# The guard of a chunk selection as a step of its own, and a new order for all steps

## The chip, the cores and the metric

The kernel runs on one core of a Trainium2 chip. The metric is the device time of one execution in microseconds; a profile of one execution shows what each engine did. The engines are TensorE (PE, with its weight loads as PEld), VectorE (DVE), ScalarE (ACT), GpSimd (POOL) and SyncE (SP, which here only issues transfers). Each works through its own queue of instructions in order and waits where an instruction needs something that another engine has not finished.

## The reference

Attention in which each query looks only at the six best chunks of 32 keys, followed by a normalised gated feed-forward layer. Batch 4, 8 heads, 768 positions, head dimension 64; model dimension 512, hidden dimension 1536:

```python
k_chunks = k.reshape(B, H, nc, chunk, D)          # 24 chunks of 32
k_min, k_max = np.min(k_chunks, axis=3), np.max(k_chunks, axis=3)
ub = np.sum(np.maximum(q[:, :, :, None, :] * k_min[:, :, None, :, :],
                       q[:, :, :, None, :] * k_max[:, :, None, :, :]), axis=-1)
ub = np.where(causal, ub, -1e9)
top_chunks = np.argsort(ub, axis=-1)[..., -6:]
scores = np.where(sel & causal_positions, scale * q @ k.T, -1e9)
x = softmax(scores) @ v                            # heads side by side: 3072 x 512
xn = x / rms(x) * rms_g
g, val = xn @ w_gate, xn @ w_val
out = (g * sigmoid(g) * val) @ w_out
```

## The kernel before, in words

**Tiling.** The 32 heads are taken as 16 pairs (two heads fill the 128 partitions). A pair goes through `prep`: q and k are loaded (qload, kload; `qnat`, `knat`), turned by TensorE (qT, kT, line 517) and copied out of PSUM (qE, kE, by ACT or DVE). DVE takes each chunk's maximum and minimum of k (kmx, kmn, lines 546 and 548), their difference is taken (dif, 599), the positive part of q is taken (relu, 633 on ACT or 635 on DVE), and TensorE forms the bounds (ub, 723 or, for two pairs at once, 781), which are copied out (ubE), turned back (up) and masked (ubm).

**Selection.** Function `choose`: twelve MAX8 instructions (max, line 650) give the eight largest bounds of each query; the sixth is the threshold. `pick` (step sel) writes, into 25 columns, whether each of 24 chunks beats the threshold (lines 665, 674), and in the 25th the guard: the largest bound minus 480, not under zero (lines 668, 679). Both instructions are one step on DVE. For the first three pairs (a0, a1, a2) the 25 columns stand in a tile `selq` and are turned by TensorE (selT, 694) and copied into the tile `qs` (selC); for later pairs they stand in `qn` beside a bf16 copy of q (qN, on GpSimd) and both are turned by a transposing transfer (qX, line 557). The columns of k that face them are constants, so that one matmul gives the score plus the mask.

**Attention and the feed-forward part.** Scores (sc, 868) go through the exponential on ACT (exp, 885), for batches 1 to 3 through a causal mask on GpSimd (mask, 891), then to the product with v (av, 904), which DVE normalises (xb, 924 and 925). Every half batch of 384 rows is normalised (`norm`: sq, eps, root, xs, then tp and tpE, or transfers xT) and multiplied by the gate weights (gate, line 1037), the value weights (val, 1058) and the output weights (po, 1078), with tanh on ACT (1044) and two DVE instructions for each of the twelve hidden slices (tg 1050, hh 1066). poE copies the output out and out stores it.

**What sets the order.** Nothing is scheduled when the kernel is built. `PROGRAM` is a string written out ahead: each word names the engine (P, A, D, G, S), the number of the step, and the buffer slots it opens. `Order.run` gives each step that engine and slot, and the steps are emitted in that sequence, so each engine's queue is the words with its letter. The durations given to `add` only served the search that wrote the string. Steps named busy (line 338) are optional: matmuls on a tile of zeros, of which the string holds 34, the first 12 in front of TensorE's first transpose. GpSimd's queue also issues the loads of v and of the weights (wg, wv, wo, lines 437 and 442).

In PROGRAM the first pairs' steps are known by number only; here they are named by the kind of step and the pair, as relu of a4. Each pair has a set (tiles `ke` and `qs`), of which there are three; a pair's copies of k into `ke` (kC) wait until the scores of the set's earlier pair are done.

Of the kernel before, what the change touches and what calls it, by code (L numbers as in the profile page):

```python
# [21 lines left out]
GUARD = 480.0  # L22
# [176 lines left out]
def kernel(  # L199
# [83 lines left out]
    def pe(n):  # L283
        return 0.003 + n / 2400.0
# [56 lines left out]
    for i in range(BUSY):  # L341
        bank = Buf("ps")
        add("busy", "PE", pe(4 * P), 1000.0 + i, busy(bank, 4 * P), [c_zero], opens=[bank])
# [135 lines left out]
    def prep(c, i0, nb, at, lr):  # L479
# [162 lines left out]
        def choose(last, ubm, m8):  # L642
# [43 lines left out]
            if side_q:  # L686
                c.sel = turned(QN, qn, QS, "qX", [pk, qs_n])
                return c.sel
# [461 lines left out]
```

## Time and profile before

| | |
|---|---|
| median of 3 runs | 315.69 us (314.5 to 319.53) |
| the profiled execution | 314.75 us, span 313.0 us |
| PE busy | 303.2 us (97%) |
| DVE busy | 231.5 us (74%) |
| ACT busy | 185.5 us (59%) |
| GpSimd busy | 103.9 us (33%) |
| mean granted TensorE clock | 0.997 |

The span runs from the first to the last instruction; the time of the execution has a little around it. In the timeline rows the first number is the start in us, the second the length of the run of instructions, and what stands in brackets is the idle time of the engine before it and who ended it. In the rows of groups the number behind x is the count; behind the bar stand the busy time in us, the mean of one in ns, and the idle time in front of the group. Busy time of matmuls is partly modelled: one matmul's end overlaps the next one's start, so spacing is the better price.

### The profile page before, as it was taken

The page shows a single profiled execution, that of the slowest core. Times are in us where ns is not written, and L with a number is a line of the kernel's source. Part 1 is how long each engine was busy: PE and PEld are TensorE (multiplying, and loading weights), DVE is VectorE, ACT ScalarE, POOL GpSimd, SP SyncE. Part 2 cuts the span into 40 slices and gives each one's busy share as a digit, 9 for nine tenths or more (in the row PEclk, how much of TensorE's full clock was granted, in tenths as well). Part 3 has the DMA queues.
Part 4 walks back from the last instruction along what each step waited for, and adds up shares of the span by engine and source line. Part 5 has one row for each costly group of instructions (what it writes and reads, how often), then busy time and mean ns, then how long its engine had stood idle before and what let it go on. Part 6 is the DMA issues. An engine that isn't in the chain of part 4 may idle for free.

```text
span 313.0 us, 7431 instructions
## 1 busy us (share of the span) xinstructions
PE 303.2 (97%) x2772; PEld 191.7 (61%) x2790; DVE 231.5 (74%) x654; ACT 185.5 (59%) x415; POOL 103.9 (33%) x162
## 2 busy tenths in 40 slices
PE   7998999999999999999999999999999999999994
PEld 3676776576576855667687546656666545555541
DVE  4998989969985789856978879989544564577551
ACT  1688998783298773697794643366697403442001
POOL 8686453371354843252377100033233110000000
PEclk9999999999999999999999999999999999999998
DMA  9999999999699996797684060361240034100014
GB/s 173 220 190 126 96 191 206 201 165 168 129 185 198 220 114 146 175 191 138 138 68 28 17 140 13 52 77 36 58 79 36 2 78 155 69 3 0 2 67 169
DMA packets 113301, 35.35 MB, mean 113 GB/s; under 512 B 106225, under 2 KB 110065, under 8 KB 113265
## 3 DMA queue, kind: packets, MB, share of 16 engines
q1 hardware_dynamic: 83152, 26.62, 41.1%
q0 software_dynamic: 28512, 7.87, 24.9%
q10 hardware_dynamic: 1600, 0.39, 0.6%
q8 instruction: 22, 0.36, 0.5%
q14 instruction: 15, 0.11, 0.1%
HBM read 28.57 MB, written 6.29 MB: 111 GB/s over the span
## 4 chain that ended last, share of the span: by engine, by line
PE 87%; DMA 5%; DVE 4%; POOL 1%; issue 1%; SPq 1%; ACT 1%; POOLq 0%
PE po L1078 20%; PE vp L1058 19%; PE gp L1037 19%; PE sc L868 9%; PE av L904 5%; DMA wv<-in_moe_w_val_dram 4%; PE pk L517 3%; PE busy L338 3%; PE pq L517 3%; PE ub L781 2%; PE ub L723 2%; PE up L803 1%; DMA qs<-qn 1%; DVE m L650 1%; DVE qs L293 1%
## 5 line engine op out<-in xcount | busy, mean ns | idle before, releaser
L885 ACT ACTIVATE pt<-sc 128x512 bf16<-128x512 f32 (+2 forms) x192 | 92.9, 561 | 17.5 <-PE sc L868 15.4
L1044 ACT ACTIVATE sg<-gp 128x384 bf16<-128x384 f32 x96 | 45.5, 496 | 55.1 <-PE gp L1037 42.2
L1050 DVE SCALAR_TENSOR_TENSOR tg<-sg,gp 128x384 bf16<-128x384 bf16 x96 | 51.8, 550 | 32.0 <-ACT sg L1044 30.6
L1058 PE MATMUL vp<-xT,wv 128*128 128x384 bf16 x384 | 74.0, 326 | 0.3 <-DMA wv<-in_moe_w_val_dram 0.2
L1037 PE MATMUL gp<-xT,wg 128*128 128x384 bf16 x384 | 73.2, 326 | 0.7 <-ACT xT L289 0.4
L1078 PE MATMUL po<-wo,hh 128*128 128x512 bf16 x272 | 66.9, 379 | 0.9 <-issue 0.2
L1066 DVE TENSOR_TENSOR hh<-vp,tg 128x384 bf16<-128x384 f32 x96 | 51.6, 552 | 12.6 <-PE vp L1058 11.7
L868 PE MATMUL sc<-qs,ke 128*128 128x128 bf16 (+5 forms) x420 | 57.1, 251 | 0.3 <-DMA qs<-qn 0.2
L1058 PEld LDWEIGHTS <-wv 128*128 128x128 bf16 x384 | 35.9, 98 | 25.0 <-issue 1.2
L1037 PEld LDWEIGHTS <-wg 128*128 128x128 bf16 x384 | 36.2, 98 | 23.9 <-issue 1.5
L1078 PEld LDWEIGHTS <-hh 128*128 128x128 bf16 x288 | 27.3, 98 | 29.1 <-issue 1.5
L904 PEld LDWEIGHTS <-pt 128*128 128x128 bf16 x672 | 35.1, 98 | 10.5 <-ACT pt L885 0.6
L904 PE MATMUL av<-vx,pt 128*128 128x65 bf16 x672 | 41.4, 193 | 0.1
L891 POOL TENSOR_SCALAR_AFFINE_SELECT pt<-pt 128x512 bf16<-128x512 bf16 (+1 forms) x48 | 24.4, 521 | 47.4 <-ACT pt L885 43.6
L868 PEld LDWEIGHTS <-ke 128*128 128x128 bf16 (+1 forms) x420 | 30.6, 97 | 9.6 <-issue 1.6
L293 POOL CAST ke<-kt 64x768 bf16<-64x768 f32 x32 | 26.6, 835 | 16.6 <-ACT kt L289 6.0
L293 POOL CAST qn<-qnat 128x768 bf16<-128x768 f32 x13 | 10.7, 822 | 40.5 <-DMA qs<-qn 40.5
L291 ACT ACTIVATE osb<-po 128x512 f32<-128x512 f32 x12 | 7.1, 599 | 24.7 <-PE po L1078 24.7
L981 DVE SCALAR_TENSOR_TENSOR xs<-xb,ri,gains 128x512 bf16<-128x512 bf16 x24 | 17.5, 751 | 2.1 <-POOL ri L973 1.7
L925 DVE TENSOR_TENSOR xb<-av,rden 128x384 bf16<-128x384 f32 (+1 forms) x34 | 18.2, 534 | 1.2
L473 POOL DMA_DIRECT2D vx<-in_v_dram x16 | 16.9, 1055 | 0.1
L650 DVE MAX8 m<-ubm 128x8 f32<-128x8 f32 (+4 forms) x192 | 16.7, 160 | 0.2
(83 smaller groups left out, 297.7 us busy)
## 6 DMA issues: line engine op xcount, KB each, us to landing
out_dram<-osb SPq DMA_DIRECT2D x24, 256.0 KB, 2.3
knat<-in_k_dram SPq DMA_DIRECT2D x30, 192.0 KB, 4.3
qnat<-in_q_dram SPq DMA_DIRECT2D x30, 192.0 KB, 4.6
vx<-in_v_dram POOLq DMA_DIRECT2D x16, 192.0 KB, 5.5
wg<-in_moe_w_gate_dram POOLq DMA_DIRECT2D x2, 768.0 KB, 11.6
wv<-in_moe_w_val_dram POOLq DMA_DIRECT2D x2, 768.0 KB, 10.0
wo<-in_moe_w_out_dram POOLq DMA_DIRECT2D x2, 768.0 KB, 10.1
qs<-qn SPq DMA_TRANSPOSE x26, 2.8
```

What stands on the lines that cost most here:

```text
L293: engine[e].tensor_copy(out_, in_)
L650: nc.vector.max(out=m8.tile[:, y[0], y[1], :], in_=ubm.tile[:, y[0], y[1], 0:max(8, 4 * (i0 + x) + 4)])
L868: nc.tensor.matmul(t[:, x:x + m, :].rearrange("p a b -> p (a b)"), ke[kk, kb * P:(kb + 1) * P], qs[kk, q0 * P:(q0 + m) * P], start=not tri ...
L885: nc.scalar.activation(out=t[:, 0:nn, :], in_=sc.tile[:, 0:nn, :], func=ACT.Exp, scale=SCALE)
L891: nc.gpsimd.affine_select(out=pt.tile[:, 0:nd, :], in_=pt.tile[:, 0:nd, :], compare_op=ALU.is_ge, fill=0.0, base=0, pattern=[[0, nd], [1, ...
L904: nc.tensor.matmul(av.tile[:, qi - i0, :], pt.tile[:, x, :], VX[c.v.slot][:, hl * NT + kb, :], start=(begin and m == 0), stop=(left[0] == ...
L1037: nc.tensor.matmul(t[:], wg[:, g, hs], XT[b].tile[:, g, cols], start=(g == 0), stop=(g == NP - 1))
L1044: nc.scalar.activation(out=t[:], in_=gp.tile[:], func=ACT.Tanh, scale=0.5)
L1050: nc.vector.scalar_tensor_tensor(out=t[:], in0=sg.tile[:], scalar=1.0, in1=gp.tile[:], op0=ALU.add, op1=ALU.mult)
L1058: nc.tensor.matmul(t[:], wv[:, g, hs], XT[b].tile[:, g, cols], start=(g == 0), stop=(g == NP - 1))
L1066: nc.vector.tensor_tensor(out=t[:], in0=vp.tile[:], in1=tg.tile[:], op=ALU.mult)
L1078: nc.tensor.matmul(po.tile[:], hhs[ht].tile[:, th * P:(th + 1) * P], wo[:, ht, :], start=(ht == 0), stop=(ht == NHT - 1))
```

## The change

The guard becomes a step (grd) of its own. `pick` keeps the comparison; `guard` writes the 25th column, on ScalarE (relu with a bias tile `cap` holding -480), on GpSimd or on DVE. What turns the selection waits for both steps. The relu of q may also go to GpSimd. PROGRAM is written anew for all steps:

```diff
+    cap = const.tile([P, 1], FP32, name="cap")
+    c_cap = add("cap", "DVE", 0.07, -98, lambda e: nc.vector.memset(cap[:], -GUARD))
...
-                nc.vector.tensor_scalar(out=t[:, 0:n], in0=big["q"].tile[:, 0:n], scalar1=0.0,
+                engine[e].tensor_scalar(out=t[:, 0:n], in0=big["q"].tile[:, 0:n], scalar1=0.0,
                                         scalar2=None, op0=ALU.max)
...
-        rl = add("relu", "", {"DVE": 0.07 + n * 0.00056, "ACT": act(n)}, ...
+        rl = add("relu", "", {"DVE": 0.07 + n * 0.00056, "ACT": act(n), "POOL": pool(n)}, ...
...
-                    nc.vector.tensor_scalar(
-                        out=s12[:, :, NCH:NCH + 1], in0=m12[:, :, 0:1], scalar1=-GUARD,
-                        scalar2=0.0, op0=ALU.add, op1=ALU.max)
...
+            def guard(e):
+                if side_q:
+                    s12 = QN[qn.slot][:, D:D + 2 * NT * P].rearrange("p (t d) -> p t d", d=P)
+                    m12 = m8.tile[:].rearrange("p h i e -> p (h i) e")
+                else:
+                    s12 = SELQ[sq.slot][:, 0:nb].rearrange("p i h e -> p (i h) e")
+                    m12 = m8.tile[:, 0:nb].rearrange("p i h e -> p (i h) e")
+                o, m = s12[:, :, NCH:NCH + 1], m12[:, :, 0:1]
+                if e == "ACT":
+                    nc.scalar.activation(out=o, in_=m, func=ACT.Relu, bias=cap[:, 0:1])
+                else:
+                    engine[e].tensor_scalar(out=o, in0=m, scalar1=-GUARD, scalar2=0.0,
+                                            op0=ALU.add, op1=ALU.max)
+
+            gd = add("grd", "", {"ACT": 0.22, "POOL": 0.25, "DVE": 0.12}, rank(at, b, "sel"), guard,
+                     last + (c_qn if side_q else c_sel) + [c_cap], opens=[qn if side_q else sq], uses=[m8],
+                     port=True)
-            pk = add("sel", "DVE", 0.18 + nb * 48 * 0.00104, ...
+            pk = add("sel", "DVE", 0.09 + nb * 48 * 0.00104, ...
...
-                c.sel = turned(QN, qn, QS, "qX", [pk, qs_n])
+                c.sel = turned(QN, qn, QS, "qX", [pk, gd, qs_n])
...
-            sT = add("selT", "PE", nb * 0.057, rank(at, b, "selT"), sel_turn, [pk, c_idb], ...
+            sT = add("selT", "PE", nb * 0.057, rank(at, b, "selT"), sel_turn, [pk, gd, c_idb], ...
```

Where the two strings give steps to engines differently:

| step | before | after |
|---|---|---|
| guard (16) | with sel on DVE | ACT 3, GpSimd 9, DVE 4 |
| relu (16 pairs) | ACT 12, DVE 4 | ACT 6, DVE 4, GpSimd 6 |
| kE and qE (64) | ACT 46, DVE 18 | ACT 39, DVE 25 |
| ubE (22) | ACT 17, DVE 5 | ACT 12, DVE 10 |
| kC (32) | GpSimd 32 | GpSimd 30, ACT 2 |
| dif (16) | GpSimd 11, DVE 5 | GpSimd 12, DVE 4 |
| selC (3) | DVE 3 | DVE 2, ACT 1 |
| ke0, the constants of the first set | DVE | ACT |
| tpE (6) | ACT 4, DVE 2 | ACT 3, DVE 3 |
| busy on PE | 34, twelve ahead of the first transpose | 26, six ahead of it |

In the early part the new string loads the first half of a0's k ahead of its q; takes the third and the fourth pair's k in the other order; and on GpSimd's queue has, between the load of the fourth pair's v and the first weight load, the guard of a2, qN and two kC of a6, two kC of a3, the relu of a4 and one kC of a4, while the other kC and the qN of a4 stand behind the first three weight loads. Before, that place held qN of a6, kC of a2, both kC of a4 and qN of a4.

More of the change, by code (lines that the diff above doesn't have):

```diff
@@ L634, in relu @@
             else:
-                nc.vector.tensor_scalar(out=t[:, 0:n], in0=big["q"].tile[:, 0:n], scalar1=0.0,
+                engine[e].tensor_scalar(out=t[:, 0:n], in0=big["q"].tile[:, 0:n], scalar1=0.0,
                                         scalar2=None, op0=ALU.max)
-        rl = add("relu", "", {"DVE": 0.07 + n * 0.00056, "ACT": act(n)}, rank(at, b, "relu"), relu, done["q"], opens=[rel],
+        rl = add("relu", "", {"DVE": 0.07 + n * 0.00056, "ACT": act(n), "POOL": pool(n)}, rank(at, b, "relu"), relu, done["q"], opens=[rel],
                  uses=[big["q"]], port=True)
@@ L678, in pick @@
                     op0=ALU.max, op1=ALU.is_gt)
-                nc.vector.tensor_scalar(
-                    out=s12[:, :, NCH:NCH + 1], in0=m12[:, :, 0:1], scalar1=-GUARD,
-                    scalar2=0.0, op0=ALU.add, op1=ALU.max)
-            pk = add("sel", "DVE", 0.18 + nb * 48 * 0.00104, rank(at, b, "sel"), pick,
+            def guard(e):
[14 more added lines that the diff above has]
+                     port=True)
+            pk = add("sel", "DVE", 0.09 + nb * 48 * 0.00104, rank(at, b, "sel"), pick,
                      last + (c_qn if side_q else c_sel), opens=[qn if side_q else sq], uses=[m8, ubm],
@@ L696, in sel_turn @@
                         ident_b[:])
-            sT = add("selT", "PE", nb * 0.057, rank(at, b, "selT"), sel_turn, [pk, c_idb], opens=[st], uses=[sq])
+            sT = add("selT", "PE", nb * 0.057, rank(at, b, "selT"), sel_turn, [pk, gd, c_idb], opens=[st], uses=[sq])
             def sel_out(e):
```

247 rows, old and new, of the table PROGRAM are left out of this document.

## The prediction

> **What bounds the kernel now.** I read the share of busy time first, then the busy time of four stretches cut at the first real matmul, the first gate matmul and the last matmul.
>
> ```profile
> PE 303.2 (97%) x2772; PEld 191.7 (61%) x2790; DVE 231.5 (74%) x654; ACT 185.5 (59%) x415; POOL 103.9 (33%) x162
> ```
>
> ```profile
> 0.00:7.27 7.27, 5.07 (x13) 1.87 (x13) 3.26 (x10) 1.49 (x2) 6.15 (x17) 1.00 0.92 170
> 7.27:51.19 43.92, 42.13 (x568) 31.10 (x569) 39.67 (x121) 37.05 (x83) 25.47 (x39) 1.00 1.16 169
> 51.19:308.94 257.75, 255.96 (x2194) 158.69 (x2209) 188.52 (x525) 146.32 (x329) 72.24 (x107) 1.00 0.59 101
> 308.94:313.00 4.06, 0.05 (x1) 0.00 (x0) 0.00 (x0) 0.60 (x1) 0.00 (x0) 0.76 0.51 190
> ```
>
> After the stretch and its length stand PE, PEld, DVE, ACT and POOL busy. From 51.19 us to the last matmul PE idles 1.79 us of 257.75: there the work of TensorE itself is the limit, and a new order can only tie or lose. The last 4.06 us are the last eviction and its transfer. What an order can win lies before 51.19 us, where PE is kept full partly by fillers, matmuls on zeros (line 338):
>
> ```profile
> 2.20 5.24 PE L338 MATMUL busy<-zeros 128*128 128x512 bf16 x12 [2.20 <-DVE zeros L333]
> 7.27 0.49 PE L517 MATMUL pk<-ident_f,knat 128*128 128x128 f32 x3
> ...
> 8.58 1.46 PE L338 MATMUL busy<-zeros 128*128 128x512 bf16 x6
> ...
> 38.47 0.66 PE L868 MATMUL sc<-qs,ke 128*128 128x128 bf16 x7
> ...
> 40.10 0.40 PE L868 MATMUL sc<-qs,ke 89*128 89x128 bf16 x4 [0.18 <-DMA qs<-qn]
> ...
> 51.19 2.76 PE L1037 MATMUL gp<-xT,wg 128*128 128x384 bf16 x16
> ```
>
> The first twelve fillers take 5.07 us, some 0.42 us each; a later one takes 0.216 us (six in 1.46, the last counted with its modelled end of 0.38). The program has 34, so 22 later ones stand for 4.8 us that PE had nothing to do. Without any filler PE's work is 303.2 - 5.07 - 4.8 = 293.3 us. Put behind a start at 4.8 us (below) and ahead of the tail of 4.06, that is a span of 302.2: no order gets under that, so 10.8 us is all there is to win.
>
> What holds PE back before the gates is the chain of waits:
>
> ```profile
> 34.02 0.52 PE st L694 x6
> 34.55 0.07 issue
> 34.62 0.83 POOL ke L293
> 35.45 1.75 SPq L557
> 37.20 0.05 issue
> 37.25 2.80 DMA qs<-qn
> ...
> 40.25 0.85 POOL qn L293
> ...
> 41.87 0.70 POOL wg L437
> 42.57 11.57 DMA wv<-in_moe_w_val_dram
> ```
>
> Two things hang on the selection here. The transposes of the fourth pair's q with its selection (line 557) leave when DVE has written the selection, and the last scores of the first batch start at 40.10, when they have landed. And GpSimd's cast into the same buffer (qn, 40.25) waits for those transposes and stands in front of the weight loads, so wg leaves at 41.87 and wv, 11.57 us later, is the last thing the first products need. DVE's rows around it:
>
> ```profile
> 31.14 1.00 DVE L650 MAX8 m<-ubm 128x8 f32<-128x8 f32 x12
> ...
> 33.16 0.81 DVE L679 TENSOR_SCALAR selq<-m 128x12 bf16<-128x12 f32 x1
> ...
> 34.23 0.19 DVE L668 TENSOR_SCALAR qn<-m 128x12 bf16<-128x12 f32 x1
> ...
> 44.54 0.36 DVE L925 TENSOR_TENSOR xb<-av,rden 128x192 bf16<-128x192 f32 x1
> ```
>
> DVE is busy 39.67 of 43.92 us there and ACT 37.05: the early stage is bound by these two, in turns, and its length is what I try to size.
>
> **The change part by part.** Only the early stage is summed; steps are named by pair (a0 the first). Prices:
>
> ```profile
> L679 DVE TENSOR_SCALAR selq<-m 128x12 bf16<-128x12 f32 x3 | 2.4, 812 | 0.0
> L668 DVE TENSOR_SCALAR qn<-m 128x12 bf16<-128x12 f32 x13 | 2.9, 225 | 0.0
> L346 DVE MEMSET selq<- 128x384 uint32 x2 | 0.8, 378 | 0.1
> L293 DVE COPY qs<-st 64x768 bf16<-64x768 bf16 x6 | 3.3, 555 | 0.6 <-PE st L694 0.5
> L293 DVE COPY qt<-pq 128x384 f32<-128x384 f32 x9 | 4.9, 551 | 1.8 <-PE pq L517 1.8
> L635 DVE TENSOR_SCALAR rt<-qt 128x768 f32<-128x768 f32 x4 | 2.2, 552 | 0.1
> L599 DVE TENSOR_TENSOR ku<-kmx,ku 128x24 f32<-128x24 f32 x5 | 1.0, 192 | 0.0
> L289 ACT ACTIVATE qt<-pq 128x384 f32<-128x384 f32 x23 | 10.8, 495 | 1.0 <-PE pq L517 0.6
> L633 ACT ACTIVATE rt<-qt 128x768 f32<-128x768 f32 x12 | 10.3, 860 | 2.0 <-PE ub L781 1.7
> L330 ACT ACTIVATE first<-ident_f 128x1 f32<-128x1 f32 x1 | 0.2, 204 | 0.0
> L293 POOL CAST qn<-qnat 128x768 bf16<-128x768 f32 x13 | 10.7, 822 | 40.5 <-DMA qs<-qn 40.5
> L891 POOL TENSOR_SCALAR_AFFINE_SELECT pt<-pt 128x512 bf16<-128x512 bf16 x24 | 15.2, 637 | 21.5 <-ACT pt L885 17.9 <-PE av L904 3.5
> ```
>
> *The guard.* The same small instruction costs 0.812 us in the first pairs and 0.225 later. The three dear ones run while GpSimd does its casts of 0.82 us, so I read the difference of 0.59 as DVE held by GpSimd. The Trainium skill (GPSIMD Engine Reference, Key points) has a rule for it: GpSimd shares its SBUF interfaces with VectorE and contends with DVE instructions that use both ports or have two SBUF inputs. The trace agrees by 0.812 against 0.225, and the rule speaks against giving GpSimd more work; what it would cost is the third rival.
>
> *The start.* In the new order the first k is loaded ahead of q, and 6 fillers instead of 12 stand before its transpose.
>
> ```profile
> 0.81 0.99 SPq L497 DMA_DIRECT2D qnat<-in_q_dram  x2
> 1.84 2.66 SPq L497 DMA_DIRECT2D knat<-in_k_dram  x4
> ```
>
> ```profile
> DMA to landing us min/median/max: 3.5/4.3/5.5
> ```
>
> The landing row is that of knat. The first half of k would be issued at 0.81 instead of 1.84 and land at 4.3 to 6.3; the fillers would end at 2.20 + 6 x 0.42 = 4.7, so its transposes move from 7.27 to between 4.8 and 6.3. The second half is still the fourth load and gains only the fillers ahead. I take 1.4 us for the whole start, between 0 (if the second pair's k, still the fifth load, decides) and 2.4.
>
> *DVE up to the fourth pair's selection* (34.42, the end of the row at 34.23). Gone from this stretch: one memset 0.38, two copies of the first pair's selection that ACT takes 1.11, three dear guards 2.44 (a1 to ACT, a2 to GpSimd, a0 stands apart again and is added below), one cheap guard 0.23 (a3, to ACT): 4.16. Added: the first pair's relu 0.55 and difference 0.19, a small memset 0.11, two evictions of q 1.10, the guard of a0, between 0.225 and 0.812: I take 0.81, the row of the same place. Sum 2.76, net 1.4 earlier (2.0 with the cheap guard). With the start, 2.8 us: selection at 31.6, fourth pair's scores at 37.3 instead of 40.10.
>
> *ACT between its first exponential and the last one that the first norm needs*: 40 exponentials in both orders; one relu (0.86), two evictions of q (0.99) and one of k (about the same 0.5) go, a guard of 0.2 (the row of the smallest activation) comes: 2.15 less. The first pair's selection copies, now ACT's, stand ahead of it and are dearer there than DVE's 1.11; they eat part of the start's 1.4, about 0.5. So ACT is 3.0 earlier, near DVE's 2.8. The guards of a1 and a3 stand among the exponentials and wait for DVE's maxima; the a1 guard stands directly in front of the first exponential, where a late maximum would hold the whole row of them.
>
> *GpSimd up to the weights.* The second cast of q that waited until 40.25 is now behind the weight loads. In front of them stand instead: the guard of a2, one qn cast, four ke casts, the relu of a4 and a ke cast that waits for the third pair's scores. A relu of 128x768 on GpSimd is in no row: the cast of as many elements is 0.82, the masks' 0.637 for 512 gives 0.96 for 768, and twice the cast, 1.64, is the far end I take; under 0.637, the shorter mask, nothing speaks. I take 0.85, beside the cast. A guard is between 0.2 and 0.82. The a2 guard waits for the maxima that ended at 32.14 in the old order, 29.3 by my sum; 0.25 + 0.82 x 6 + 0.85 on top is 35.4. The scores it needs are PE's 24.2 us of work in, reached around 39 us in the old order (the row at 38.47), 36.2 now, and a cast of 0.83 later the weights leave: 37 instead of 41.87. wv lands at about 49.4 instead of 54.14.
>
> *First gate.* The last needed attention output ends at 44.90 (row 44.54) and the gates follow 6.3 us later by an unchanged sequence of squares, root, scaling, four transposes and evictions. 2.8 earlier gives 48.4, and the weights are then there (wg before 47, wv when the third group asks for it at 49.7, which also saves the 0.24 of wait at 54.19). PE has exactly the same 140 real steps before it in both orders, so it can follow.
>
> *The rest.* PE's work is the same. DVE gets seven evictions and five smaller copies more but twelve guards fewer, about nothing in sum; ACT loses six relus and twelve evictions, about 6 us of 146, under PE's cover; GpSimd gains six relus, nine guards and loses two casts, 5.9 us on 103.9, also covered unless DVE is held. On SP's queue the transposes keep their sequence but for pairs that change places, and loads of later pairs shift by a place or two. I allow 0.6 us for new waits beside the 1.79.
>
> Sum: -2.8 - 0.24 + 0.6 = -2.4. The profiled execution took 314.75 us, its span 313.0 and 1.75 around it: 310.6 + 1.75 = **312.3 us**. The median of the runs shown, 315.69, lies 0.94 above the profiled one, and they spread from 314.5 to 319.53, so about 2% is what tells a change from none.
>
> **The rivals.** *The early gain does not arrive.* The loads, not the engines, set the pace: DMA's busy share is 1.16 in the early stretch by the row above, the loads after the fourth come in nearly the old sequence, and a front that is only 1 us earlier then meets the same landings. Or the maxima for the guards come late and hold ACT and GpSimd. For it: the dense DMA row. Against: DVE idles only 4.25 us in that stretch, so it, not the loads, was mostly late. It gives 313.0 + 0.6 + 1.75 = 315.3, between 314 and 317.
>
> *Nearly all fillers close.* The start gains its 2.4 and DVE its 2.0, the 0.24 goes, and the 1.79 of later idle time closes too: 314.75 - 6.4 = 308.3; the floor of 302.2 above is a time of 304.0. For it: a front that long is idle only through fillers. Against: start, DVE, ACT and every later wait must come right at once.
>
> *DVE becomes the bound: slower.* By the shared port each DVE instruction that meets a GpSimd one may take 0.59 more. The place is where DVE is fullest while GpSimd now has relus and guards:
>
> ```profile
> 150.00:200.00 50.00, 49.79 (x438) 31.96 (x439) 43.72 (x109) 30.28 (x68) 16.30 (x24) 1.00 0.42 62
> ```
>
> DVE has 6.28 us to spare there; eleven holdings use it up, and each further one is 0.59 on PE. To be slower than before by 2% (322), the 2.4 gained and 7.25 more must be lost: 16 holdings beyond the spare. Few holdings past it give 316 to 319. For it: the three guards. Against: the 24 scalings with two SBUF inputs lie mostly beside little GpSimd work, and GpSimd is busy a third of the time.
>
> **How the numbers follow.** Forecast 312.3 (310 to 314): 0.47. No gain, 315.3: 0.25. DVE held, 316 and up: 0.18, two thirds of it over 322 or so. Fillers closed, 308.3 (304 to 309): 0.10. The 8-in-10 range is 308.5 to 319.5: about 0.06 is left out below and 0.13 above. Faster by over 2% (under 309.4): 0.10; slower by over 2% (over 322): 0.12; between: 0.78.
>
> **What would show it.** In the new profile: first real matmul near 5 us; the fourth pair's transposes issued near 32; wg issued near 37; first gate at 48 to 49; from there PE idle 2 to 3 us. Wrong if the first gate is still near 51 (the loads decide), if GpSimd's relu is far over 0.85, if scalings or squares on DVE have grown by 0.5, or if PE waits on DVE in the middle stretch.

## The result, and the profile after

The new kernel takes 312.65 us (median; 311.42 to 314.49) against 315.69 for the kernel before in the same series: a ratio of 0.9925, with a 95% interval of 0.9898 to 0.9951. Each ratio here is taken over the runs within 1.5% of their kernel's fastest, so where the runs of a kernel scatter it lies below the ratio of the medians. That is a gain of three quarters of a per cent, within the 2% that is called no change, and beside the forecast of 312.3. The profiled execution took 312.63 us, its span 310.9 against 313.0.

Share of busy time of the new kernel, then four stretches cut as before at the first real matmul, the first gate matmul and the last matmul (after the stretch and its length stand PE, PEld, DVE, ACT and POOL busy):

```profile
PE 300.8 (97%) x2764; PEld 190.4 (61%) x2782; DVE 232.2 (75%) x651; ACT 182.2 (59%) x405; POOL 119.5 (38%) x176
```

```profile
0.00:3.79 3.79, 2.55 (x7) 0.77 (x7) 2.56 (x8) 0.82 (x1) 2.98 (x10) 1.00 0.54 119
3.79:48.99 45.20, 42.61 (x567) 31.14 (x567) 37.88 (x122) 39.88 (x89) 32.56 (x47) 1.00 1.28 184
48.99:307.07 258.08, 255.66 (x2194) 158.46 (x2209) 191.75 (x522) 140.94 (x316) 83.97 (x121) 1.00 0.60 100
307.07:310.90 3.83, 0.02 (x1) 0.00 (x0) 0.00 (x0) 0.60 (x1) 0.00 (x0) 0.95 0.55 203
```

Against the four lengths of before (7.27, 43.92, 257.75, 4.06) the span's 2.1 us come apart as follows: the first real matmul is 3.48 earlier, the way from it to the first gate is 1.28 longer, the rest up to the last matmul 0.33 longer, the tail 0.23 shorter. So by this cut the gain is made at the very start, and a third of it is given back before the gates; what the start carries by itself, an experiment shows below. The timeline of PE in the new kernel shows where:

```profile
1.24 2.74 PE L339 MATMUL busy<-zeros 128*128 128x512 bf16 x6 [1.24 <-DVE zeros L334]
3.79 0.87 PE L520 MATMUL pk<-ident_f,knat 128*128 128x128 f32 x3
...
6.03 0.86 PE L520 MATMUL pq<-ident_f,qnat 128*128 128x128 f32 x3 [0.51 <-DMA qnat<-in_q_dram]
...
20.75 0.52 PE L520 MATMUL pk<-ident_f,knat 128*128 128x128 f32 x3 [1.28 <-DMA knat<-in_k_dram]
...
42.09 0.52 PE L520 MATMUL pk<-ident_f,knat 128*128 128x128 f32 x3 [0.42 <-DMA knat<-in_k_dram]
...
48.99 1.46 PE L1051 MATMUL gp<-xT,wg 128*128 128x384 bf16 x8
51.90 0.82 PE L1072 MATMUL vp<-xT,wv 128*128 128x384 bf16 x4 [1.45 <-DMA wv<-in_moe_w_val_dram]
```

Behind the fillers every wait in these rows is for a load: q of a0, k of a6, k of a5, and 1.45 us for the value weights, where the kernel before waited 0.24. DVE, GpSimd and the transfer queue of SP in the same kernel, around the selection and the weights:

```profile
31.70 0.61 DVE L668 SCALAR_TENSOR_TENSOR qn<-m,ubm 128x288 bf16<-128x288 f32 x1
...
41.75 0.36 DVE L939 TENSOR_TENSOR xb<-av,rden 128x192 bf16<-128x192 f32 x1
```

```profile
31.17 0.82 POOL L294 CAST qn<-qnat 128x768 bf16<-128x768 f32 x1
33.05 3.35 POOL L294 CAST ke<-kt 64x768 bf16<-64x768 f32 x4 [1.06 <-PE sc L888]
36.49 2.14 POOL L638 TENSOR_SCALAR rt<-qt 128x768 f32<-128x768 f32 x1
38.57 0.82 POOL L294 CAST ke<-kt 64x768 bf16<-64x768 f32 x1
39.34 0.82 POOL L440 DMA_DIRECT2D wg<-in_moe_w_gate_dram  x1
```

```profile
32.47 3.31 SPq L560 DMA_TRANSPOSE qs<-qn  x2
35.82 1.17 SPq L500 DMA_DIRECT2D qnat<-in_q_dram  x2
37.04 1.27 SPq L500 DMA_DIRECT2D knat<-in_k_dram  x2
```

The selection of a3 is written at 32.31 (34.42 before), its transposes leave at 32.47, and the last attention output that the first norm needs ends at 42.11 (44.90 before). The relu of a4 on GpSimd takes 2.14 us, not 0.85, and stands in front of the first weight load, which leaves at 39.34. SP issues a5's k by 38.31, one microsecond ahead of the weights. That microsecond turned out to matter. The groups (mean ns of one behind the bar and the busy time):

```profile
L638 POOL TENSOR_SCALAR rt<-qt 128x768 f32<-128x768 f32 x6 | 12.8, 2134 | 10.6 <-ACT qt L290 6.1 <-DVE qt L294 4.3
L638 DVE TENSOR_SCALAR rt<-qt 128x768 f32<-128x768 f32 x4 | 2.7, 674 | 0.0
L691 POOL TENSOR_SCALAR qn<-m 128x12 bf16<-128x12 f32 x8 | 3.5, 434 | 28.5 <-DVE m L653 26.8 <-ACT kt L290 1.7
L689 ACT ACTIVATE qn<-m,cap 128x12 bf16<-128x12 f32 x2 | 0.7, 355 | 0.0
L691 DVE TENSOR_SCALAR qn<-m 128x12 bf16<-128x12 f32 x3 | 0.6, 184 | 0.0
L995 DVE SCALAR_TENSOR_TENSOR xs<-xb,ri,gains 128x512 bf16<-128x512 bf16 x24 | 17.2, 751 | 3.1 <-POOL ri L987 2.9 <-DMA xT<-xs 0.2
```

### The profile page after: what moved, and what is told of

The parts are those of the page before. It is cut to its first block, busy times and chain, and to the rows that moved or that the text cites. A ratio compares the mean times of both kernels' runs of the same rounds, so it can differ in the third digit from the quotient of the medians.

```text
span 310.9 us, 7415 instructions
## 1 busy us (share of the span) xinstructions
PE 300.8 (97%) x2764; PEld 190.4 (61%) x2782; DVE 232.2 (75%) x651; ACT 182.2 (59%) x405; POOL 119.5 (38%) x176
## 4 chain that ended last, share of the span: by engine, by line
PE 87%; DMA 8%; POOL 2%; ACT 1%; issue 1%; ACTq 0%; SPq 0%; POOLq 0%
PE vp L1072 20%; PE po L1092 20%; PE gp L1051 19%; PE sc L882 10%; PE av L918 6%; DMA wg<-in_moe_w_gate_dram 5%; PE pq L520 3%; PE pk L520 3%; PE ub L795 2%; DMA knat<-in_k_dram 2%; PE ub L737 1%; DMA qnat<-in_q_dram 1%; POOL ke L294 1%; PE up L817 1%; PE busy L339 1%; POOL rt L638 1%
## 5 line engine op out<-in xcount | busy, mean ns | idle before, releaser
L899 ACT ACTIVATE pt<-sc 128x512 bf16<-128x512 f32 (+1 forms) x192 | 94.0, 556 | 21.2 <-PE sc L882 18.4
L1051 PE MATMUL gp<-xT,wg 128*128 128x384 bf16 x384 | 74.2, 326 | 0.1
L882 PE MATMUL sc<-qs,ke 128*128 128x128 bf16 (+4 forms) x420 | 59.3, 251 | 0.0
L882 PEld LDWEIGHTS <-ke 89*128 89x128 bf16 (+1 forms) x420 | 31.0, 97 | 10.0 <-issue 1.4
L294 POOL CAST ke<-kt 64x768 bf16<-64x768 f32 x30 | 25.3, 846 | 7.3 <-PE sc L882 2.8
L987 POOL TENSOR_TENSOR ri<-ms,mhalf 128x3 f32<-128x3 f32 x8 | 7.2, 904 | 33.6 <-DVE ms L979 33.5
L520 PE MATMUL pk<-ident_f,knat 128*128 128x128 f32 x96 | 16.0, 282 | 1.7 <-DMA knat<-in_k_dram 1.7
L476 POOL DMA_DIRECT2D vx<-in_v_dram x16 | 17.3, 1079 | 0.1
```

The costliest lines, as they stand in the source:

```text
L294: engine[e].tensor_copy(out_, in_)
L520: nc.tensor.transpose(t[:, j * P:(j + 1) * P], nat[w].tile[:, j0 + j].rearrange("p h d -> p (h d)"), ident_f[:])
L882: nc.tensor.matmul(t[:, x:x + m, :].rearrange("p a b -> p (a b)"), ke[kk, kb * P:(kb + 1) * P], qs[kk, q0 * P:(q0 + m) * P], start=not tri ...
L899: nc.scalar.activation(out=t[:, 0:nn, :], in_=sc.tile[:, 0:nn, :], func=ACT.Exp, scale=SCALE)
L1051: nc.tensor.matmul(t[:], wg[:, g, hs], XT[b].tile[:, g, cols], start=(g == 0), stop=(g == NP - 1))
```

## The experiments

Steps are words of the program: engine letter and number. G415 is the relu of a4, G412 a copy of k of a4, G76 and G77 the first loads of wg and wv, S475 and S470 the loads of a5's q and k, S356 the first transpose of a3. Unless another base is named, the edit is made to the new kernel. Ratios are to the kernel before, run on the same chip in the same series; its medians there were 315.10 to 315.49.

### Do earlier weights pay? The loads out of GpSimd's queue

The value weights are what PE waits for after the first gate, and GpSimd's slow relu stands in front of them. The first theory was that weights sent earlier give the 1.45 us back.

```diff
+G76
+G77
 G415:1
...
-G76
...
-G77
```

> The new kernel with the first wg and wv issued ahead of the relu of a4 on GpSimd; everything else in its place, so that relu and the ke cast behind it come 1.6 us later. Theory A: wg leaves near 36.5, wv lands near 49, PE's wait for wv is gone, 1.3 us faster: 311.3. Theory B: the landing is set by the other transfers: no change, 312.6.

Measured: 325.34 us (324.6 to 326.49), ratio 1.0321 (1.0292 to 1.035). In this kernel wg left at 35.43 and wv at 36.25, and SP's issues and PE's timeline are:

```profile
35.05 1.18 SPq L500 DMA_DIRECT2D qnat<-in_q_dram  x2
36.27 1.36 SPq L500 DMA_DIRECT2D knat<-in_k_dram  x2
37.68 6.55 SPq L432 DMA_DIRECT2D gains<-in_moe_rms_g_dram  x1
```

```profile
54.59 0.87 PE L520 MATMUL pk<-ident_f,knat 128*128 128x128 f32 x3 [13.95 <-DMA knat<-in_k_dram]
```

The weights now leave ahead of a5's k, whose two loads were issued at 36.27 and 36.9. They took 13.8 and 17.6 us from issue to landing instead of 4.1 to 4.3 in the new kernel, and PE stood still for 13.95 us waiting for them. Behind that wait the granted clock is 0.66 from 54.5 to 60 us and 1.00 from 60 to 110; a third of 5.5 us, some 1.9 us by my estimate, is lost there on top. The theory fell: what the weights gain, a load that PE needs sooner loses many times over. The next edit only makes GpSimd shorter.

```diff
-G415:1
+D415:1
```

> The new kernel with one word of the order changed: the relu of a4 on DVE (about 0.58 us) instead of GpSimd (2.13 us), where it stands in front of the weight loads. Theory A (that relu holds the weight loads back): wg leaves near 37.3 instead of 39.34, wv lands near 49.8, PE's wait of 1.45 us for wv at the first value product falls under 0.3, and the time drops by about 1.2 us, from 312.6 to 311.4. Theory B (the landing of the weights is set by the other transfers of that time): wv lands at 51.5 or later all the same and the time stays within 0.4 us of 312.6.

Measured: 316.48 us, but runs from 312.06 to 322.2; the ratio 0.9984 (0.9947 to 1.0021) stands for the seven of twelve that took 316.7 or less. The profiled run, at 313.71, shows wg issued at 37.57, while SP was still issuing a5's k (36.81 to 37.94):

```profile
43.71 0.52 PE L520 MATMUL pk<-ident_f,knat 128*128 128x128 f32 x3 [1.75 <-DMA knat<-in_k_dram]
```

The wait for wv is gone and one of 1.75 us for a5's k stands in its place; its two loads landed in 3.8 and 6.2 us, against 4.1 and 4.3 in the new kernel. The weights came earlier as the theory said; the time of neither theory fits. That the runs near 320 us are those in which the weights won is a guess, not shown: the profile holds one run.

All six relus were then taken off GpSimd and put on DVE.

```diff
-G415:1
+D415:1
```

The same is done to words 346, 486, 557, 716 and 1121.

> The new kernel with all six relus of GpSimd on DVE. Theory A (only the one in front of the weights costs time, the others lie under PE): the same as with that one alone, 311.4 within 0.5 us. Theory B (GpSimd's long relus hold DVE through a shared port and so stretch the order): another 1 to 2 us on top, 310 or less. Theory C (DVE is too full to take 3.4 us more): slower than with one relu moved, 312 to 313.

Measured: 332.34 us (327.25 to 338.73). No theory had foreseen it. PE waits in this kernel for loads and transposes, the longest here:

```profile
67.83 1.14 PE L882 MATMUL sc<-qs,ke 89*128 89x512 bf16 x6 [4.93 <-DMA qs<-qn]
```

Beside it stand 2.29 us for k at 46.24 and 2.59 for q at 77.20, and two issues of q held SP for 7.57. All idle time of PE comes to 14.2 us here against 5.1 in the new kernel, while the span is 17.3 longer (328.2). The other half is slower work: PE is busy for 309.6 us against 300.8, and the granted clock is 0.77 from 47 to 53 us, 0.53 from 67.8 to 74 and 0.76 from 77 to 84, behind these three waits. The six slow relus cost less where they stand than their absence does. That this is again a matter of loads that meet is argued from these waits; which load met which was not followed further.

If the race with a5's loads is the cause, those loads sent ahead of a3's transposes should settle it.

```diff
+S475:6
+S470:1
 S356:0
...
-S475:6
...
-S470:1
```

> The new kernel with the loads of q and k of the pair a5 issued ahead of the transposes of the fourth pair's q on SP's queue, so at about 25.5 us instead of 35.8 to 38.3, when their buffers are free and SP only waits. Theory A (these loads and the weights, which leave 1 us behind them at 39.34, compete for the same transfer engines): PE's wait of 0.42 us for a5's k is gone, wv lands 0.5 to 1 us earlier than 51.9, the spread between runs does not grow, time 311.5 to 312.2 against 312.65. Theory B (only the order on each queue counts): 0.4 us from the wait for k, wv as before, 312.2. Against both: the loads now delay earlier ones, PE waits for a k or q before 35 us, time over 313.

Measured: 312.33 us, with runs only 1.6 us apart (311.31 to 312.94), ratio 0.9903 (0.988 to 0.9927). Its interval and the new kernel's overlap, so the 0.2% between them is not clear of noise. The wait for a5's k is gone, and the value weights are late by half as much:

```profile
50.84 0.82 PE L1072 MATMUL vp<-xT,wv 128*128 128x384 bf16 x4 [0.67 <-DMA wv<-in_moe_w_val_dram]
```

On top of this edit, the weights were again put ahead of the relu (the two edits together).

> The same with wg and wv also issued ahead of the relu of a4, near 35.4 instead of 39.34. The kernel with the weights ahead alone took 325.3 us, with PE waiting 13.95 us for a5's k. Theory A (that loss was the race of a5's loads against the weights, which wins now by 8 us): no wait for a5's k, no wait of 1.45 us for wv, 310 to 311.2. Theory B (weights that leave early hold back whatever load is behind them): another transfer takes its place with a wait of several us, 315 or more.

Measured: runs from 310.48 to 322.54, median 315.75; the ratio 0.9856 (0.9826 to 0.9886) stands for the three of twelve that took 311.4 or less. What the nine at 315.37 and above waited for is not recorded. In the profile there is no 14 us wait for k any more, which shows that the order of those two issues caused it. But wg at 35.41 now meets a3's transposes, issued to 35.5, and the scores wait for them:

```profile
38.62 0.27 PE L882 MATMUL sc<-qs,ke 89*128 89x128 bf16 x2 [1.77 <-DMA qs<-qn]
```

Two milder versions on top of the same early loads followed: the relu of a4 on DVE (D415 for G415), and G76 and G77 one place up, between G415 and G412.

> Edit: the new kernel with a5's loads of q and k ahead of a3's transposes, and the relu of a4 on DVE instead of GpSimd. Theory A (the spread of the kernel with the relu of a4 on DVE came from the weights meeting a5's loads; here those are out of the way): wg issued near 37.5, no wait for a5's k and none for wv, first gate 49 to 49.5, time 311 to 312.5 with runs no further apart than 3 us. Theory B (the relu, 0.6 to 1.0 longer on the full DVE, or the weights meeting a3's transposes instead, causes the spread): wait for qs<-qn at the scores of a3, or several runs over 315, median 313 or more.

> Edit: the new kernel with a5's loads of q and k ahead of a3's transposes, and the first wg and wv moved one place up on GpSimd's queue, ahead of the copy of k of a4 (behind its relu). Theory A (0.8 us earlier weights fill the 0.67 us that PE still waits for wv, and nothing else moves): wg issued near 38.6, no wait at the first products of wv, time 311.3 to 312.2. Theory B (a second later issue still meets a3's transposes, which end about 36.5, and the loads behind): median over 313 or several runs over 315.

Measured: 311.55 us (310.86 to 312.39), ratio 0.9881 (0.9856 to 0.9906), for the relu on DVE; 312.11 (311.96 to 313.85), ratio 0.9904 (0.988 to 0.9928), for the other. In the first, GpSimd's and PE's timelines:

```profile
36.64 0.82 POOL L440 DMA_DIRECT2D wg<-in_moe_w_gate_dram  x1
```

```profile
49.18 1.46 PE L1051 MATMUL gp<-xT,wg 128*128 128x384 bf16 x8
50.48 0.81 PE L1072 MATMUL vp<-xT,wv 128*128 128x384 bf16 x4
```

No wait stands before the value products; from the first gate on PE has no idle time worth a row. The same relu on DVE whose twelve runs spread over 10 us without the early loads has six runs within 1.5 here, so DVE's extra 0.55 us alone does not make the spread; the race with a5's loads, which is what the other edit takes away, is the likely cause, and no profile of a long run shows it. For the wait at a3's scores theory B was right in part: 1.32 us at 38.45 in this kernel, 1.19 at 38.54 in the other, and the time came out low all the same. The relu on DVE with early loads has the lowest median of the study, 1.2% under the kernel before (of the three shortest runs of the kernel above alone the ratio is lower); that it beats the new kernel is likely but not certain, since their intervals touch (0.9906 and 0.9898).

### What is the start worth?

The front was put back: a0's q ahead of its k, the memset of the zeros in its old place, twelve fillers in front of the first transposes.

```diff
-S83:0
 S88:1
 S89
+S83:0
...
-D3
...
+D3
...
+P10:7
+P11:0
+P12:2
+P13:5
+P14:7
+P15:6
 P86:6
...
-P10:7
...
-P11:0
...
-P12:2
...
-P13:5
-P14:7
...
-P15:6
```

> The new kernel with the front of the old order: first q and then k of a0, the memset of the zeros behind those of qn, twelve fillers ahead of the first transpose. Theory A (the earlier start is a term of the gain and is carried to the end): the first real matmul at 7 us instead of 3.79, the first gate 1.4 to 3.4 us later than 48.99, time 314 to 316. Theory B (the start is swallowed by later landings, such as PE's wait of 1.28 us for k at 20.75): within 0.5 us of 312.65.

Measured: 314.92 us (313.14 to 316.52), ratio 0.9985 (0.9963 to 1.0006). PE's timeline of this kernel:

```profile
6.95 0.52 PE L520 MATMUL pk<-ident_f,knat 128*128 128x128 f32 x3
...
49.62 1.46 PE L1051 MATMUL gp<-xT,wg 128*128 128x384 bf16 x8
53.16 1.12 PE L1072 MATMUL vp<-xT,wv 128*128 128x384 bf16 x4 [2.08 <-DMA wv<-in_moe_w_val_dram]
```

The start is worth about 2 us (2.3 by the medians, 1.9 by the ratios), most of the gain. In the one profile the first matmul is 3.16 later, but the selection of a3 only 0.52 (32.83), the last attention output 0.43 (42.54) and the first gate 0.63: most of a later start is absorbed in front of the gates. The first value product is 1.26 later, since the wait for wv grows from 1.45 to 2.08. Directly behind that wait the two kernels differ once more, this kernel in the first row, the new one in the second, with the granted clock as the third number from the end:

```profile
53.20:60.00 6.80, 6.80 (x32) 3.65 (x33) 3.41 (x7) 1.96 (x4) 0.23 (x2) 0.75 1.36 144
53.20:60.00 6.80, 6.73 (x48) 4.04 (x46) 5.63 (x11) 4.14 (x9) 2.99 (x2) 1.00 1.19 183
```

In 6.8 us PE does 32 matmuls instead of 48. A quarter of these 6.8, some 1.7 us by my estimate, goes to the lower clock, which is 1.00 in both kernels from 60 us on. So the two profiled spans, 2.7 us apart, come apart as 0.6 at the first gate, 0.6 more of waiting for wv, and a rest of 1.4 that the clock behind it about accounts for. Why the clock falls behind this wait and not behind the shorter one is not shown.

### What is the guard worth?

In the old kernel the guards of a0, a1 and a2 alone were given to ACT, with no step moved; the tile `cap` and its memset, 0.06 us on DVE, come with them.

```diff
-                nc.vector.tensor_scalar(
-                    out=s12[:, :, NCH:NCH + 1], in0=m12[:, :, 0:1], scalar1=-GUARD,
-                    scalar2=0.0, op0=ALU.add, op1=ALU.max)
+                nc.scalar.activation(out=s12[:, :, NCH:NCH + 1], in_=m12[:, :, 0:1],
+                                     func=ACT.Relu, bias=cap[:, 0:1])
```

> The old kernel with one thing changed: the guards of a0, a1 and a2, which cost DVE 0.81 us each, are computed by ScalarE at the same place of the order. Theory A (each frees 0.81 us on DVE, the bound engine of the early stage): the fourth pair's selection is written about 2 us earlier than 34.42, the first gate comes at 49 to 50 instead of 51.19, time 313 to 314 against 315.1. Theory B (DVE is held by GpSimd's casts, and the next DVE instruction that needs the shared port takes the wait instead): the comparisons of those pairs stay at 0.8 to 1.0 and the time stays within 0.5 us of 315.1.

Measured: 314.45 us (313.85 to 319.27), ratio 0.9977 (0.9956 to 0.9998). DVE's and GpSimd's timelines of this kernel:

```profile
31.58 1.07 DVE L676 SCALAR_TENSOR_TENSOR selq<-m,ubm 128x288 bf16<-128x288 f32 x1
32.57 1.07 DVE L667 SCALAR_TENSOR_TENSOR qn<-m,ubm 128x288 bf16<-128x288 f32 x1
```

```profile
31.48 0.84 POOL L293 CAST qn<-qnat 128x768 bf16<-128x768 f32 x1
32.25 1.08 POOL L293 CAST ke<-kt 64x768 bf16<-64x768 f32 x1
```

The casts end at 32.32 and 33.33, the two comparisons at 32.65 and 33.64. A comparison that falls into a cast ends 0.31 to 0.33 behind the cast's end, whenever it began; alone it takes 0.45. In the new kernel the same: the cast ends at 31.99, the comparison at 32.31. So the hold is real, but it is not the guard's: with the guard gone, the next comparison takes its place in the second cast and grows to 1.07. The selection was written at 33.76 instead of 34.42, the first gate came at 50.27 instead of 51.19, and 0.7 (by the ratio) to 1.0 us (by the median) came of it, with an interval that ends just short of no change.

The other way round, the twelve guards that the new kernel has on ACT and GpSimd were put on DVE behind their comparisons, so that all sixteen are there.

```diff
-A179:1
-D180
+D180:1
+D179
```

Words 247, 354, 494, 588, 594, 735, 729, 876, 870, 1011 and 1017 are moved in the same way.

> The new kernel with the guard's split undone: all sixteen guards on DVE, each directly behind its comparison, the order otherwise kept. Theory A (the split's gain lies in the first pairs, where a guard cost 0.81 us on DVE): the guards of a1 and a2 cost 0.4 to 0.8 each, that of a3 0.2, the first gate comes 0.5 to 1.5 us later than 48.99, time 313 to 314. Theory B (the guard's place is worth nothing, the new order brought the gain): within 0.4 us of 312.6, guards at 0.19 each.

Measured: 315.12 us (314.02 to 319.1), ratio 0.9998 (0.9973 to 1.0023). The whole gain was gone, more than either theory allowed. To see where, the first three alone were put on DVE (179, 247 and 354).

> Edit: the new kernel with the guards of a1, a2 and a3 alone back on DVE behind their comparisons; the nine late ones stay on ACT and GpSimd. Theory A (what twelve guards on DVE lost is lost in the first stage, where a small DVE instruction is held while GpSimd casts): three guards of 0.2 to 0.8 us, so the selection of a3 is written about 1 us later, the first gate is at 49.7 to 50.3, the time 314 to 315. Theory B (the loss came from the nine late guards): first gate within 0.3 of 48.99, time 312.3 to 313.2.

Measured: 312.92 us (311.74 to 313.54), ratio 0.9916 (0.9891 to 0.9941): as good as the new kernel. DVE's timeline in this kernel:

```profile
30.89 0.45 DVE L668 SCALAR_TENSOR_TENSOR qn<-m,ubm 128x288 bf16<-128x288 f32 x1
31.25 0.19 DVE L691 TENSOR_SCALAR qn<-m 128x12 bf16<-128x12 f32 x1
```

In the new order the early guards cost 0.19 on DVE, and the first gate came at 48.49. Moving them off DVE is worth nothing there. So the nine late ones had to carry the loss, and all twelve were measured again.

> Edit: the same twelve guards on DVE as in the first such kernel, taken again because its profile fell in a disturbed run and because the first three guards alone on DVE cost nothing. Theory A (the nine late guards on DVE lose 2 to 3 us): ratio again between 0.997 and 1.002, and waits of PE behind 60 us, of the kind of the 2.54 us for qs<-qn at 85.93. Theory B (the first measurement was spoiled by its surroundings; where the guard stands is worth nothing): ratio 0.990 to 0.994, first gate within 0.5 of 48.5, no wait over 0.5 us behind 60 us.

Measured: 315.58 us (314.1 to 319.35), ratio 1.0014 (0.9983 to 1.0044), the loss again, and the predicted wait: the timelines of PE, GpSimd and SP of this kernel, and the landing times of its transposes in 74 to 82 us (shortest, median, longest):

```profile
84.20 0.38 PE L882 MATMUL sc<-qs,ke 128*128 128x128 bf16 x4 [3.34 <-DVE tg L1064]
```

```profile
74.84 2.04 POOL L476 DMA_DIRECT2D vx<-in_v_dram  x2
84.21 0.82 POOL L294 CAST qn<-qnat 128x768 bf16<-128x768 f32 x1 [7.33 <-DMA qs<-qn]
```

```profile
75.99 2.91 SPq L560 DMA_TRANSPOSE qs<-qn  x2
```

```profile
DMA to landing us min/median/max: 6.4/6.6/6.7
```

The same views of the kernel with only the three early guards on DVE, GpSimd's, SP's and the landing times:

```profile
78.55 0.31 POOL L691 TENSOR_SCALAR qn<-m 128x12 bf16<-128x12 f32 x1 [3.99 <-DVE m L653]
78.99 2.09 POOL L476 DMA_DIRECT2D vx<-in_v_dram  x2
```

```profile
75.51 2.55 SPq L560 DMA_TRANSPOSE qs<-qn  x2
```

```profile
DMA to landing us min/median/max: 2.5/2.6/2.7
```

With the guard (that of a6, word 588) on GpSimd, the load of v behind it in the queue waits until 78.99, when the transposes of q issued from 75.51 are nearly through. Without the guard the load of v leaves at 74.84, just ahead of the transposes, and these take 6.4 and 6.7 us to land instead of 2.5 and 2.7. PE's scores wait 3.34 us. (Its row names DVE's tg as the last to come, but GpSimd's cast, which waits for the same transposes, starts at 84.21; in the first such run the row of that place named the transposes.) The late guards are worth their 3 us together, and the one that the traces show at work is worth it because it waits, and the load of v with it; the other eight were not taken one by one.

## Why the prediction was right, and where it was not

- **What bounds the kernel: right.** PE idles 2.42 us of 258.08 behind the first gate (1.79 before), and the whole gain lies ahead of it.
- **The start: right place, another way.** The first real matmul came at 3.79, under the 4.8 to 6.3 forecast, because the zeros are also written earlier, so the fillers begin at 1.24 instead of 2.20, and because the first k lands sooner than I bounded. Put back, it costs about 2 us. But I had 1.4 us of the start arrive at the selection and at the last attention output, and by the profile with the old front only 0.52 and 0.43 of it do, 0.63 at the first gate. The rest of the 2 us is a longer wait for wv and the lower clock behind it, which were in no term.
- **DVE up to the selection: right sum, wrong reading.** The selection is written at 32.31, 2.11 earlier and not 2.8; the last attention output ends 2.79 earlier (2.8 forecast). Without the start's 0.43 that is 2.36 from everything else, where the sum had 1.4 for it and 1.4 for the start: two errors that offset each other, which is luck. The term also counted 2.44 us for three dear guards gone from DVE. The runs show that a guard costs DVE 0.19 wherever no cast stands beside it, and that a hold passes to the next comparison where one does. With the early guards put back on DVE in the new order, neither they nor the comparisons beside them are held in the profile (0.45 to 0.46 each comparison). So the holds went because the casts fall elsewhere, not because the guards left; a0's guard, which I took at 0.81, cost 0.19.
- **ACT: right.** Its first square for the norm starts at 42.15 instead of 45.05. The guard in front of the first exponential did not hold them: it took 0.35 where I allowed 0.2, with no idle time behind it.
- **GpSimd up to the weights: wrong.** This is the step that failed. The relu, priced 0.85 beside the cast with 1.64 as its far end, takes 2.14, so the weights left at 39.34 and not at 37, and PE waited 1.45 us for wv where I had the wait vanish. The relu holds them 1.8 us: with it on DVE they left at 37.57. By my own sum 2.14 would still have been covered (36.7, under the 37 that the scores set); but the maxima ended at 30.59 and not at 29.3, and the queue waited 1.06 us at 33.05 for scores that the sum left out. GpSimd's busy time rose by 15.6 us over the whole, where I had 5.9. The step was also wrong in its direction: it took earlier weights as a gain, and five kernels show that weights sent ahead of a5's k, or beside a3's transposes, cost 1.2 to 14 us of waiting, which two of them got back in all their runs and a third in three of twelve. I did not ask what the weights collide with.
- **First gate 48.4, came 48.99.** The 0.6 too much lie between the last attention output and the gate, 6.88 us where I took 6.3.
- **The rest: 0.6 of new waits.** Behind the gate PE idles 2.42 us where the sum had 1.79 - 0.24 + 0.6 = 2.15. But 1.45 of it is the wait for wv, which the sum had vanish, so the other waits came to 0.97 where it had 2.15.
- **The rivals.** The early gain did arrive, though the load of wv still holds PE behind the gates. The fillers did not all close. DVE did not become the bound: the scalings stay at 751 ns and no wait for DVE stands in the middle. The real danger to the gain, transfers that meet, was in my list only as loads that land late, not as loads that leave too early.

So the place of the gain was forecast, and the time was hit to 0.4 us with luck. The first gate came 0.6 later than the sum has it and PE idled 0.27 more behind it, against a tail 0.23 shorter and PE's work behind the gate 0.30 shorter, which stood in no term. And ahead of the gate less of the start than its term arrived, while the rest of the early stretch gave more than its own.

## What to carry to other kernels

Where one in-order queue computes and also issues loads, each of its instructions sets when a transfer starts; before taking a slow step out of it, or a waiting one, list which transfers then leave earlier and what they meet. In this kernel weight loads issued four microseconds earlier made 325 us of 312. So put the small loads that are needed soon ahead first (here a5's), and shorten the queue only after that. And price an operation that the trace does not show by its own kind on that engine: a cast said nothing of a relu.

## What the runs showed of the hardware

- A relu of 128x768 in fp32 takes 2134 ns on GpSimd, where a cast of as many elements takes 825, and 674 on DVE. The Trainium skill (GPSIMD Engine Reference, section 4.1, Engine selection) calls one-input elementwise work on GpSimd "roughly line-rate"; the measurement, 3.2 times DVE's, decides against it for this form. The 128x12 guard takes 434 ns on GpSimd, 355 on ACT, 184 on DVE.
- A DVE comparison that begins while GpSimd casts ends about 0.32 us after the cast does, so the hold is set by what is left of the cast (casts ending at 32.32, 33.33 and 31.99, comparisons at 32.65, 33.64 and 32.31); alone it takes 0.45. Six MAX8 at 26.88 beside a cast (26.74 to 27.57) in the new kernel took 0.57, as six without a cast did at 30.02.
- The two loads of one pair's k took 13.8 and 17.6 us instead of 4.1 and 4.3 when two weight loads of 768 KB were issued at 35.43 and 36.25 and those of k at 36.27 and 36.9. The Trainium skill (DMA: Bandwidth & Descriptors, Queues, rings and completion order) says that each DMA engine goes round its queues packet by packet. That a queue of small packets gets the smaller share by this is my inference; the long landing agrees with it, the share itself was not measured.
- The granted clock fell behind some long waits of PE and not behind others: 0.66 for 5.5 us behind 13.95 in the kernel with the weights ahead, 0.53 for 6.2 us behind 4.93 in the kernel without relus on GpSimd, 0.75 for 6.8 us behind 2.08 with the old front, but 1.00 behind 3.34 with the late guards on DVE and behind 1.45 in the new kernel. No rule follows from these.
